# Three fp32 sums over partitions turned into pairs of rounded products, with their splits moved ahead, in an adaLN linear-attention block

## The chip, the cores and the metric

The kernel runs on one NeuronCore of a Trainium2 chip. The metric is the device time of one execution, in microseconds; less is better. Before the change it is 563.58 us, the median of three runs that lie between 562.93 and 564.28.

## What is computed

A block of a transformer with 2048 tokens of width 512: a condition vector `c` gives six modulation vectors; then come a linear attention with 32 heads of width 16 and a bilinear feed-forward of width 1376, each behind a layer norm that is scaled and shifted by its modulation and each added to `x` through a gate (`ga`, `gb`).

```
mod = silu(c) @ w_mod                      # six vectors of 512: sa, ca, ga, sb, cb, gb
h = layernorm(x) * (1 + ca) + sa
q, k, v = h @ wqkv                         # per head
phi(t) = where(t > 0, t + 1, exp(t)) + 1e-6
kv = sum_s phi(k) v ;  z = sum_s phi(k)    # over all tokens
o = (phi(q) kv) / (phi(q) z + 1e-6)
x = x + ga * (o @ wo)
h = layernorm(x) * (1 + cb) + sb
x = x + gb * (((h @ w_gate) * (h @ w_up)) @ w_down)
```

Three of these quantities are sums over the 128 partitions that are wanted as a row, the same on every partition: the gates `ga` (modulation vector 2) and `gb` (vector 5), and `z`.

## The kernel before, in words

Nearly all matrix products run in the type fp32r, which TensorE rounds: each operand is split in a high part (its rounding, made by a copy on ScalarE) and a low part (the difference, made by a subtraction on VectorE), and a product is the sum of three matmuls, high by high, high by low and low by high (`split` L192, `split_raw` L196, `product` L202). A tensor is worked on in tiles of 128 tokens by 512 columns; there are NT = 16 of them in four chunks.

The order of each engine's queue is written out by hand: an instruction stands in its engine's queue where the Python code calls it, and each engine works through its queue in that order. The loop at L612 (`for i in range(4, NT)`) is the key stage. Step i puts in the queues, among other things:

- TensorE: the projection of tile i+2 on the key weights (or, in the last two steps, of tiles 4 and 5 on the query weights), twelve matmuls (`proj` L301, lines 206 to 208); then the twelve matmuls of `t_tile(i)` (L350, lines 355 to 357), which add `x^T phi(k)` of tile i to four banks `tacc` that stay open through the whole loop.
- ScalarE: the high part of the next tile's normalized input (`k_split_x`, L193), the high part of phi(k) of tile i+1 (`k_split`, L346), and two activations on the projection (`phi_a`, L310 and L311).
- VectorE: the two low parts (L194 and L347), the end of phi (`phi_b`, L314), and the running sum of phi(k) over tiles in `zacc` (`z_add`, L338 and L340).
- `extra[i]` (L552 to L562), the work that doesn't belong to the tile: splits of other weights, and the modulation vectors 2 to 5. For one vector, `mod_load` fetches four pieces of `w_mod`, `mod_part` (L547, working in `mod_acc` L166) multiplies each by a column of silu(c) and adds it to an accumulator `accs[v]` on VectorE (L169, L171), and what is left is a sum over the 128 partitions. Vectors 3 and 4 are wanted as columns (`mod_col` L173, eight matmul records with one moving column, then `col_out`). Vectors 2 and 5 are wanted as rows: `mod_row` L184 multiplies a 128x128 matrix of ones by the accumulator in one plain fp32 matmul (L186), which the trace shows as two records, and ScalarE copies the bank (L188).

In the last step, 15, `z` is made in the same way at L654, one fp32 matmul of the ones by `zacc`, and ScalarE adds a constant (L656) to give `zb`. It stands on TensorE between the projection of query tile 5 and `t_tile(15)`; `mod_row(5)` stands behind `t_tile(15)`.

After the loop, VectorE has in its queue: `phi_b` of query tile 5 (L314), two operations on `zb` (L670, L671), two products and sums for the denominators (L676, L682), four operations that finish the four banks `tacc` (L739, from copies by ScalarE at L738), and the four low parts of these (L194). TensorE goes on with the projections of query tiles 6 and 7 and then takes the product of these four tiles with the value weights into `kvps` (L749, lines 206 to 208 with 128 columns).

Buffers come from one pool of 99 tiles that are handed out again when their last reader is done, so that a load or a write can wait for an older tile's reader; loads are all issued in order on the queue of SyncE.

## Time and profile before

| what | value |
|---|---|
| median of three runs | 563.58 us (562.93 to 564.28) |
| the profiled execution, its own time | 561.47 us |
| the profiled execution, span of the instructions | 559.8 us |
| TensorE (PE) busy | 551.9 us, 99% of the span, 2544 instructions |
| VectorE (DVE) busy | 379.8 us, 68% |
| ScalarE (ACT) busy | 294.2 us, 53% |
| GpSimd (POOL) busy | 207.4 us, 37% |
| DMA | 57.24 MB, mean 102 GB/s |

PE and PEld are TensorE's matmuls and weight loads, DVE is VectorE, ACT ScalarE, POOL GpSimd and SP the engine that issues the loads. `L186` is line 186 of the kernel. In a line of the timeline stand the start in us, the duration, the engine, the line and operation, the tile written and the tiles read (without numbers), the shapes, the number of instructions put together, and in brackets how long the engine stood idle before it and what it waited for. Matmuls are pipelined: two of them start 0.23 us apart though each is shown with 0.39 us, so that costs on TensorE are read from starts. The chain of waits goes back from the last instruction, at each step to the one that released it.

### The profile page before, as it was taken

To read this page: it belongs to the slowest core of one execution; us is meant where nothing else is said; L and a number is where in the kernel's file an instruction comes from. 1 tells how busy PE (TensorE), PEld (TensorE's weight loads), DVE (VectorE), ACT (ScalarE), POOL (GpSimd) and SP (SyncE) were. 2 spreads that over 40 slices of the span, in tenths; PEclk is the share of its full clock that TensorE was granted. 3 is DMA by queue.
4 is the path that set the end of the run, shared out by engine and by line. 5 is a ranking of instruction groups with operands and counts; after the bars stand their busy time and mean duration, and the time that the engine had idled before them with its cause. 6 is when DMAs were issued, how large, how long until landed. Compare 5 with 4: busy or idle time off the path is not lost.

```text
span 559.8 us, 7391 instructions
## 1 busy us (share of the span) xinstructions
PE 551.9 (99%) x2544; PEld 453.5 (81%) x2544; DVE 379.8 (68%) x648; ACT 294.2 (53%) x531; POOL 207.4 (37%) x226
## 2 busy tenths in 40 slices
PE   7999999999999999999999999999999999999997
PEld 5888888888888888888888888878888888888775
DVE  5968779869898998865655766862455545444653
ACT  3876858446476877663545355553444334334420
POOL 2000000003327646343556644485424455554200
PEclk9999999999999999999999999999999999999999
DMA  8910224202230020151446136598353211200004
GB/s 254 384 39 1 75 76 150 77 0 71 80 114 2 0 76 0 39 159 68 150 151 195 32 122 221 178 363 286 114 157 87 57 39 48 71 0 1 0 1 150
DMA packets 50133, 57.24 MB, mean 102 GB/s; under 512 B 6384, under 2 KB 28912, under 8 KB 50096
## 3 DMA queue, kind: packets, MB, share of 16 engines
q1 hardware_dynamic: 50096, 56.77, 31.8%
q8 instruction: 20, 0.33, 0.3%
q14 instruction: 17, 0.14, 0.1%
HBM read 43.12 MB, written 13.63 MB: 101 GB/s over the span
## 4 chain that ended last, share of the span: by engine, by line
PE 94%; DVE 3%; DMA 1%; SPq 0%; issue 0%; ACT 0%; POOL 0%
PE bank L970 38%; PE acc L807 8%; PE acc L1048 7%; PE acc L1049 7%; PE acc L1050 7%; PE bank L206 5%; PE bank L207 5%; PE bank L208 5%; PE acc L357 2%; PE acc L355 2%; PE acc L356 2%; PE bank L271 2%; PE acc L439 1%; DMA x<-in_A_x_dram 1%; PE bank L782 1%; PE acc L271 1%
## 5 line engine op out<-in xcount | busy, mean ns | idle before, releaser
L970 PE MATMUL bank<-h,w 128*128 128x512 f32 (+1 forms) x924 | 215.8, 390 | 0.0
L970 PEld LDWEIGHTS bank<-h,w 128*128 128x128 f32 (+1 forms) x924 | 170.8, 185 | 38.6 <-issue 0.4
L976 ACT ACTIVATE bank<-bank 128x512 f32<-128x512 f32 (+1 forms) x44 | 25.6, 581 | 151.2 <-PE bank L970 151.1
L956 POOL TENSOR_TENSOR w<-raw,w 128x256 fp32r<-128x256 f32 (+3 forms) x44 | 46.1, 1048 | 157.2 <-ACT w L949 150.0
L996 DVE TENSOR_TENSOR phi<-bank,g 128x512 f32<-128x512 f32 (+1 forms) x22 | 15.1, 688 | 83.5 <-PE bank L970 79.8
L1048 PE MATMUL acc<-w,kh 128*128 128x512 f32 (+1 forms) x176 | 68.6, 390 | 0.0
L1049 PE MATMUL acc<-w,kh 128*128 128x512 f32 (+1 forms) x176 | 68.6, 390 | 0.0
L1050 PE MATMUL acc<-w,kl 128*128 128x512 f32 (+1 forms) x176 | 68.5, 389 | 0.0
L956 POOL TENSOR_TENSOR w<-t,w 128x512 fp32r<-128x512 f32 (+1 forms) x44 | 57.4, 1305 | 0.0
L1055 DVE TENSOR_TENSOR x<-acc,x 128x512 f32<-128x512 f32 x80 | 50.3, 681 | 8.6 <-PE acc L1050 8.6
L206 PE MATMUL bank<-w,h 128*128 128x512 f32 x112 | 44.8, 400 | 0.0
L208 PE MATMUL bank<-w,h 128*128 128x512 f32 x112 | 43.7, 390 | 0.0
L207 PE MATMUL bank<-w,h 128*128 128x512 f32 x112 | 43.6, 390 | 0.0
L676 POOL TENSOR_TENSOR f<-h,zb 128x512 f32<-128x512 f32 x12 | 17.1, 1439 | 67.8 <-ACT zb L656 49.2
L249 POOL TENSOR_TENSOR rstd<-ve,half 128x4 f32<-128x4 f32 (+3 forms) x12 | 11.2, 930 | 83.0 <-DVE ve L246 71.4
L807 PE MATMUL acc<-w,xh 128*128 128x512 f32 x128 | 40.7, 399 | 0.0
L1048 PEld LDWEIGHTS acc<-w,kh 128*128 128x128 f32 (+1 forms) x176 | 33.0, 188 | 7.1
L1050 PEld LDWEIGHTS acc<-w,kl 128*128 128x128 f32 (+1 forms) x176 | 33.0, 188 | 7.0
L1049 PEld LDWEIGHTS acc<-w,kh 128*128 128x128 f32 (+1 forms) x176 | 33.1, 188 | 6.9
L938 POOL TENSOR_TENSOR t<-raw,t 128x256 f32<-128x256 f32 (+1 forms) x44 | 36.9, 838 | 1.7
L1022 DVE TENSOR_TENSOR g<-bank,u 128x512 f32<-128x512 f32 (+1 forms) x22 | 15.2, 691 | 27.0 <-ACT u L976 27.0
L264 ACT ACTIVATE n<-x,nmr,rstd 128x512 f32<-128x512 f32 x31 | 23.7, 808 | 14.6 <-DVE nmr L254 14.4
(159 smaller groups left out, 1011.3 us busy)
## 6 DMA issues: line engine op xcount, KB each, us to landing
x<-in_A_x_dram SPq DMA_DIRECT2D x24, 256.0 KB, 5.2
raw<-in_w_mod_dram SPq DMA_DIRECT2D x24, 256.0 KB, 3.8
raw<-in_B_w_gate_dram SPq DMA_DIRECT2D x40, 128.0 KB, 3.0
raw<-in_B_w_up_dram SPq DMA_DIRECT2D x40, 128.0 KB, 3.1
raw<-in_B_w_down_dram SPq DMA_DIRECT2D x20, 256.0 KB, 3.1
side_s<-h SPq DMA_DIRECT2D x16, 256.0 KB, 2.5
h<-side_s SPq DMA_DIRECT2D x16, 256.0 KB, 5.5
out_dram<-x SPq DMA_DIRECT2D x16, 256.0 KB, 2.6
```

The costliest lines, as they stand in the source:

```text
L206: nc.tensor.matmul(ps, ah, bh, start=i == 0, stop=False)
L207: nc.tensor.matmul(ps, ah, bl, start=False, stop=False)
L208: nc.tensor.matmul(ps, al, bh, start=False, stop=i == n - 1)
L807: nc.tensor.matmul(yps[i], x, y, start=fresh and k + n == 0, stop=k == KD - 1 and n == 2, skip_group_check=True)
L938: sub = lambda out, x, y: (on or nc.gpsimd).tensor_tensor(out, x, y, op=ALU.subtract)
L956: sub = lambda out, x, y: (on or nc.gpsimd).tensor_tensor(out, x, f32(y), op=ALU.subtract)
L970: mm = lambda x, y, **kw: nc.tensor.matmul(ps, x[:, k], y, skip_group_check=True, **kw)
L976: nc.scalar.activation(out, x, AF.Copy)
L1048: nc.tensor.matmul(dn[j], hh[:n, a:b], dh[:n], start=i == 0, stop=False)
L1049: nc.tensor.matmul(dn[j], hh[:n, a:b], dl[:n], start=False, stop=False)
L1050: nc.tensor.matmul(dn[j], hl[:n, a:b], dh[:n], start=False, stop=i == n_of - 1)
L1055: nc.vector.tensor_tensor(xt, dn[j], xt, op=ALU.add)
```

## The change

It replaces the three fp32 matmuls by pairs of fp32r ones. A 128x128 matrix of ones in fp32r, `ones_r`, is made once near the start, by a VectorE copy from a column of ones (`ones` shrinks to that column). Each of the three accumulators is split in high and low like any other operand, and `over_rows` adds ones times high and ones times low in one bank. The split of vector 2 stands in step 10 (its matmuls stay in step 11), that of `zacc` in step 14, behind the last `z_add`, and that of vector 5 in step 13 (its matmuls stay in step 15); the pieces of vector 5 are worked off one earlier each (piece 0 in step 12, pieces 1 to 3 in step 13), and the first of the four `wo` tiles is split in step 13 and not in step 14. The column sums are the same instructions as before.

```diff
-    ones = consts.tile([P, P], F32, name="ones")
+    ones = consts.tile([P, 1], F32, name="ones")
     nc.gpsimd.memset(ones, 1.0)
+    ones_r = consts.tile([P, P], F32R, name="ones_r")
...
-            nc.tensor.matmul(ps[:, b:b + 1], acc[:, b * P:(b + 1) * P], ones[:, 0:1], start=True, stop=True)
+            nc.tensor.matmul(ps[:, b:b + 1], acc[:, b * P:(b + 1) * P], ones, start=True, stop=True)
...
-    def mod_row(v, acc):
+    def over_rows(ps, pair):
+        for m, x in enumerate(pair):
+            nc.tensor.matmul(ps, ones_r, x, start=m == 0, stop=m == 1)
+
+    def mod_row(v, pair):
         ps = bank()
-        nc.tensor.matmul(ps, ones, acc, start=True, stop=True)
+        over_rows(ps, pair)
...
     n0.stats(0)
+    nc.vector.tensor_copy(ones_r, ones.to_broadcast([P, P]))
     silu()
...
-             10: lambda: (mod_part(3, 0, 1, 2), mod_load(5)),
+             10: lambda: (accs.update({2: split_raw(accs[2])}), mod_part(3, 0, 1, 2), mod_load(5)),
              11: lambda: (mod_part(3, 3), mod_part(4, 0, 1), rows.update({2: mod_row(2, accs[2])})),
-             12: lambda: (raw_o.extend(load(wo_v[k], "raw") for k in range(KD)), mod_part(4, 2, 3), cols.update({3: col_out(3, mod_col(accs[3], bank()), 0.0)})),
-             13: lambda: (mod_part(5, 0, 1, 2), cols.update({4: col_out(4, mod_col(accs[4], bank()), 1.0)})),
-             14: lambda: (mod_part(5, 3), wo_s.extend(split_raw(x) for x in raw_o)), 15: lambda: rows.update({5: mod_row(5, accs[5])})}
+             12: lambda: (raw_o.extend(load(wo_v[k], "raw") for k in range(KD)), mod_part(4, 2, 3), mod_part(5, 0), cols.update({3: col_out(3, mod_col(accs[3], bank()), 0.0)})),
+             13: lambda: (mod_part(5, 1, 2, 3), wo_s.extend(split_raw(x) for x in raw_o[:1]), accs.update({5: split_raw(accs[5])}), cols.update({4: col_out(4, mod_col(accs[4], bank()), 1.0)})),
+             14: lambda: (wo_s.extend(split_raw(x) for x in raw_o[1:]),), 15: lambda: rows.update({5: mod_row(5, accs[5])})}
...
         if i + 1 < NT:
             z_add(i + 1)
+        if i + 1 == NT - 1:
+            zpair = split_raw(zacc)
...
             zps = bank()
-            nc.tensor.matmul(zps, ones, zacc, start=True, stop=True)
+            over_rows(zps, zpair)
```

More of the change, by code (lines that the diff above doesn't have):

```diff
@@ L398, in block_one @@
         at = at_of(v, b)
-        nc.tensor.matmul(sums_in(b)[:, at:at + 1], sums[v, b // 2][:, b % 2 * P:(b % 2 + 1) * P], ones[:, 0:1],
+        nc.tensor.matmul(sums_in(b)[:, at:at + 1], sums[v, b // 2][:, b % 2 * P:(b % 2 + 1) * P], ones,
                          start=True, stop=True)
```

## The prediction

> **What bounds the kernel now.** I read the page first (the span and the shares of the chain of waits), then the chain in order of time around the three sums, then the timeline there, engine by engine.

> ```profile
> span 559.8 us, 7391 instructions
> PE 94%; DVE 3%; DMA 1%; SPq 0%; issue 0%; ACT 0%; POOL 0%
> ```

> By the page TensorE sets the end nearly everywhere, so that TensorE time saved is time saved. But 3% of the chain is VectorE's, about 17 us, and the question of this change is whether its three sums lie inside or outside of that. The chain in order of time answers it (start, duration, what):

> ```profile
> 125.61 0.24 PE bank L208
> 125.85 0.02 issue
> 125.87 0.61 ACT h L310
> 126.50 0.64 ACT h L311
> 127.16 0.69 DVE h L314
> ...
> 132.13 2.65 DVE n L739 x4
> 134.78 2.42 DVE w L194 x4
> 137.20 0.04 issue
> 137.25 0.33 PE bank L207
> ```

> From 125.85 to 137.25 us the chain leaves TensorE: the projection of query tile 5 ends, ScalarE and then VectorE finish it (L310, L311, L314), VectorE does the operations on `zb` and on the four banks without a pause, and TensorE's product into `kvps` (137.25) takes up the last low part. What TensorE does in these 11.4 us is beside the chain. Two of the three sums are there, as the timeline shows:

> ```profile
> 103.59 0.39 PE L357 MATMUL acc<-kl,xh 128*128 128x512 f32 x1
> 103.82 1.02 PE L186 MATMUL bank<-f,ones 128*128 128x512 f32 x2
> ...
> 107.44 0.39 PE L355 MATMUL acc<-kh,xh 128*128 128x512 f32 x1
> ...
> 122.72 0.39 PE L357 MATMUL acc<-kl,xh 128*128 128x512 f32 x1
> ...
> 125.67 1.02 PE L654 MATMUL bank<-z,ones 128*128 128x512 f32 x2
> ...
> 129.30 1.02 PE L186 MATMUL bank<-f,ones 128*128 128x512 f32 x2
> ```

> The row for vector 2 (103.82) is before 125.85, on the chain; the one for z (125.67, behind the last L208 of that projection) and the one for vector 5 (129.30) are behind it. In the waits of the weight loads stands how close TensorE is to VectorE there:

> ```profile
> PEld bank L207 <- DVE w L194: 0.4, 2, 0.2
> ```

> TensorE arrives at `kvps` only some 0.4 us too early. Whatever it gains between 125.85 and 137 beyond what VectorE gains turns into more of this wait.

> **The price of one sum.** From the last matmul of `t_tile` to the first one behind the next projection: with the fp32 sum between, 103.59 to 107.44, 3.85 us; without one, 122.72 to 125.67, 2.95 us, which is 13 starts of 0.227. So an fp32 sum takes 0.90 us of TensorE (the slightly longer starts behind it included). Its replacement has the shape of every other matmul here, 128x128 by 128x512 in fp32r: two starts, 0.45 us. No row shows such a matmul with `ones_r`. Its bounds are 0.45 (two ordinary ones) and 0.90 (no faster than now); I take 0.45, since all the fp32r matmuls in the 2.95 us above start 0.227 apart. **Saved: 0.45 us per sum, 1.35 us in all on TensorE, of which 0.45 is on the chain.**

> **What VectorE and ScalarE must do for it.** Each split adds a ScalarE copy and a VectorE subtraction:

> ```profile
> L193 ACT ACTIVATE w<-raw 128x512 fp32r<-128x512 f32 x32 | 19.5, 625 | 4.9 <-DVE raw L1065 4.8
> L194 DVE TENSOR_TENSOR w<-raw,w 128x512 fp32r<-128x512 f32 x32 | 21.5, 684 | 5.7 <-ACT w L193 4.2 <-issue 1.5
> 104.00:125.67 21.67, 21.67 (x102) 17.75 (x102) 15.72 (x28) 9.99 (x17) 0.00 (x0) 1.00 0.00 0
> ```

> That is 3 x 0.63 = 1.9 us of ScalarE and 3 x 0.68 = 2.1 us of VectorE. The last line is the stretch from the first sum to the second: in 21.67 us VectorE is busy 15.72, ScalarE 9.99, POOL 0.00 and the DMA share is 0.00. There is room on average; what counts is the order in the queues, with these idle times in brackets:

> ```profile
> 99.38 0.73 ACT L346 ACTIVATE kh<-phi,eps_phi 128x512 fp32r<-128x512 f32 x1 [1.46 <-DVE phi L314]
> 108.94 0.69 DVE L314 SCALAR_TENSOR_TENSOR phi<-bank,phi 128x512 f32<-128x512 f32 x1 [1.56 <-ACT phi L311]
> 115.33 0.69 DVE L314 SCALAR_TENSOR_TENSOR phi<-bank,phi 128x512 f32<-128x512 f32 x1 [2.38 <-ACT phi L311]
> 117.05 1.54 DVE L171 SCALAR_TENSOR_TENSOR f<-raw,sc,f 128x512 f32<-128x512 f32 x2
> 120.43 0.60 ACT L310 ACTIVATE h<-bank 128x512 f32<-128x512 f32 x1 [3.65 <-PE bank L208]
> 121.72 0.69 DVE L314 SCALAR_TENSOR_TENSOR h<-bank,h 128x512 f32<-128x512 f32 x1 [1.86 <-ACT h L311]
> 123.59 2.49 DVE L194 TENSOR_TENSOR w<-raw,w 128x512 fp32r<-128x512 f32 x4
> 125.87 0.60 ACT L310 ACTIVATE h<-bank 128x512 f32<-128x512 f32 x1 [2.10 <-PE bank L208]
> 127.16 0.69 DVE L314 SCALAR_TENSOR_TENSOR h<-bank,h 128x512 f32<-128x512 f32 x1 [1.08 <-ACT h L311]
> ```

> *Split of vector 2 (step 10).* Its high part goes into ScalarE's idle 1.46 us ahead of 99.38. Its low part pushes VectorE's queue by 0.60 until the idle 1.56 us at 108.94 swallows it. Its matmuls come at 103.8, three microseconds later. Cost nothing; without those idle times 0.6.

> *Split of vector 5 (step 13).* This is the tightest place. ScalarE's copy stands ahead of the next tile's high parts and of L310 and waits for three multiply-adds of VectorE. With everything 0.45 earlier than before, L314 starts at 114.88 (not 115.33), `z_add` at 115.5, and the three L171 (0.74 each) end at 118.3. Until then ScalarE stands still where it now has 3.65 us idle. Then it does the high part and the two for tile 15 (0.63, 0.62, 0.72, with overlaps) until 120.1, and L310 of query tile 4, which TensorE allows at 120.43 - 0.45 = 119.98, is 0.1 late. The low parts of tile 15 come at 121.0 and are used at 125.7.

> *Split of z (step 14).* VectorE's L314 follows at 121.4, the last `z_add` ends at 122.7, ScalarE's high part at 123.35, VectorE's low part at 124.05; then the three `wo` splits that are left (0.60 apart as at 123.59, one of the four having gone to step 13) keep ScalarE until 124.95 and VectorE until 125.85. The pair for z is due at 125.67 - 0.45 = 125.22: 1.2 us spare. L310 of query tile 5 is due at 125.42 and L314 at 126.71: spare are 0.47 us on ScalarE and 0.86 on VectorE. So the start of VectorE's 10 us is set by TensorE, as now, and moves by 0.45 alone. Cost nothing; were the 0.47 used up, each further microsecond on ScalarE would be one at the end.

> *From there on.* `zb` is made by ScalarE's next instruction behind L311 (126.50), and stays there: its bank is filled well before. VectorE's stretch keeps its length, and ends 0.45 earlier. TensorE reaches `kvps` 1.35 earlier and waits 0.4 + 0.9 = 1.3 us.

> *The start.*

> ```profile
> 1.50 0.44 DVE L148 CAST w<-f 128x512 fp32r<-128x512 f32 x1
> 4.63 0.18 DVE L238 BATCH_NORM_AGGREGATE mv<-st 128x2 f32<-128x6 f32 x1
> 6.08 0.69 DVE L237 BATCH_NORM_STATS2 st<-x 128x6 f32<-128x512 f32 x1 [0.81 <-DMA x<-in_A_x_dram]
> ```

> The copy that makes `ones_r` stands behind 4.63. No row has its shape; between nothing and the 0.44 of a cast four times as wide, I take 0.15 to 0.2. VectorE waits 0.81 us for data at 6.08, so it is hidden at either end; without that wait it would cost its own length.

> *Loads and buffers.* No load is added and SyncE's order is the same. Six more tiles from the pool change whose reader the last loads of `w_mod` and the four of `wo` wait for (now, for two of them, the low part of vector 2 and the multiply behind it, by my count of VectorE's queue near 101 us); their first use is in step 12, behind the L314 at 108.94.

> ```profile
> 98.57 1.78 SPq L110 DMA_DIRECT2D raw<-in_A_wo_dram  x4
> ```

> They are issued from 98.57 to 100.35 and the last would be some 1 us later; the first `wo` split comes behind the L314 of 115.33, the others at 123. Nothing.

> **Sum.** -0.45 us: the span 559.8 becomes 559.35, the profiled execution's own time (1.67 more, 561.47) 561.02. That execution was 2.1 us under the median of the runs, so the difference is put on the median: 563.58 - 0.45 = **563.1 us**. It is 0.08%, and about 0.2% (1.13 us) is what a measurement of this kernel can tell from no change.

> **Rivals.**

> *All three count.* If VectorE's stretch shortened with TensorE's, the gain would be 1.35: 562.2 us. For it speak the chain's 94% and a 0.4 us wait so small that it may be an artefact; against it that VectorE has no gap in its stretch and starts it from L311.

> *The pair is no cheaper than fp32.* Then nothing is gained, 563.6 us. For it: no row shows it; against it, every fp32r matmul here.

> *ScalarE's queue becomes the bound (slower).* The mechanism is the wait in step 13: ScalarE stands before the high part of vector 5, and behind it stand tile 15's high parts and the two projections' L310. It decides from 0.47 us of delay on. If the two later splits ran one after the other with nothing beside them, 2 x (0.63 + 0.68) = 2.6 us would be added; less 0.47 and less the 0.45 gained, that is +1.7: 565.3 us. For it: ScalarE is blocked for 3.5 us in this step. Against: VectorE and ScalarE have their idle times in these very places, and POOL and DMA are silent there.

> *The clock closes.* The first matmuls of the execution are slower than the later ones:

> ```profile
> L153 PE MATMUL acc<-w x20: 388/582/793, 2.0 to 9.9; 128*128 128x512 f32 x20
> 2.00 6.55 PE L153 MATMUL acc<-w 128*128 128x512 f32 x18 [2.00 <-DVE w L148]
> ```

> 18 of them take 6.55 us where 18 x 0.227 = 4.1 would do: 2.5 us. If the longer wait at `kvps` brought that state back, 563.1 + 2.5 = 565.6 us. Against it: a wait of 0.4 didn't, and the 1.3 us comes in several pieces. [...]

> **How the numbers follow.** Forecast 0.63 (563.1); all three 0.14 (562.2); pair no cheaper 0.08 (563.6); ScalarE's queue 0.12 (565.3); clock 0.03 (565.6). Faster by over 0.2% means under 562.45: the second case and a little of the first by the spread of medians, 0.19. Slower means over 564.71: the last two, 0.14. Between: 0.67. The range takes the first three cases with the spread of the runs, +-0.7 us, about the likeliest, and 0.1 below the full gain: 562.1 to 564.2; the slow cases, 0.15, are left out.

> **What would show it.** Each sum as two matmuls with 0.23 between starts; L310 of query tile 5 at 125.4; VectorE without a gap from 126.7 to 136.75; `kvps` waiting for L194 for about 1.3 us, not 0.4; the same order of events 0.45 earlier from then on. I am wrong if L310 of tile 5 waits for ScalarE and not for the projection, if VectorE's stretch is shorter than 10 us, or if the pair takes other than 0.45.

## The result, and the profile after

| | before | after |
|---|---|---|
| median of 22 runs each, us | 562.91 (560.85 to 564.65) | 567.81 (560.53 to 570.24) |
| ratio of the runs after to those before | | 1.0058, 95% interval 1.0037 to 1.0078 |
| profiled execution: own time, span, us | 561.47, 559.8 | 567.49, 565.8 |
| mean granted clock of it | 1.000 | 0.988 |

The change makes the kernel slower, by 4.9 us of the medians. The ratio is smaller than the medians say, because executions more than 1.5% above the fastest, four of the 22 (569 us and more) and one each of `d_some` and `a_shift5` below, are left out of it as if they were disturbed, though they show the same fall of the clock as the others. The 22 executions fall into two groups: 17 with a mean clock of 0.990 or less (median 568.5), and five with more (median 562.1, 0.8 under before).

The page of the kernel after, its span, the granted clock in 40 slices, and the shares of the chain:

```profile
span 565.8 us, 7393 instructions
PEclk9899999999799999999999999999999999999999
PE 92%; DMA 4%; DVE 2%; SPq 0%; issue 0%; ACT 0%; POOL 0%
```

The third row is as dull as before. The second has a 7 in its eleventh slice, 141 to 156 us (40 slices of 14.1 us). What stands there in the timeline is the product into `kvps`. First what went as forecast, in the timeline from 126 us (start, duration, engine, line; in brackets the idle time before it and what ended it):

```profile
126.28 0.62 PE L187 MATMUL bank<-w,ones_r 128*128 128x512 f32 x2
126.47 0.60 ACT L315 ACTIVATE h<-bank 128x512 f32<-128x512 f32 x1 [0.52 <-PE bank L213]
126.73 0.39 PE L360 MATMUL acc<-kh,xh 128*128 128x512 f32 x1
127.77 0.69 DVE L319 SCALAR_TENSOR_TENSOR h<-bank,h 128x512 f32<-128x512 f32 x1 [0.84 <-ACT h L316]
129.45 0.62 PE L187 MATMUL bank<-w,ones_r 128*128 128x512 f32 x2
129.90 0.39 PE L211 MATMUL bank<-w,h 128*128 128x512 f32 x1
130.10 0.60 ACT L193 ACTIVATE row<-bank 128x512 f32<-128x512 f32 x1 [1.78 <-PE bank L187]
135.32 2.49 DVE L199 TENSOR_TENSOR w<-n,w 128x512 fp32r<-128x512 f32 x4
```

Each pair takes 0.45 us of TensorE (126.28 to 126.73, 129.45 to 129.90). ScalarE still waits for the projection of query tile 5 (0.52 us to spare), VectorE for ScalarE (0.84). Then the waits of the weight loads (us in total, how often, the longest):

```profile
PEld bank L212 <- DVE w L199: 1.3, 4, 0.8
PEld bank L978 <- DMA h<-side_s: 0.9, 2, 0.6
```

The first is the wait at `kvps`, 0.4 us before. Now the same two microseconds by two in both kernels (the stretch, TensorE's busy time and matmuls, the granted clock, DMA). Before:

```profile
134.00:136.00 2.00, 2.00 (x12) 1.00 0.14 33
136.00:138.00 2.00, 1.90 (x15) 1.00 0.90 224
138.00:140.00 2.00, 2.00 (x21) 1.00 0.94 238
```

After:

```profile
134.00:136.00 2.00, 1.56 (x8) 1.00 0.30 77
136.00:138.00 2.00, 1.79 (x10) 1.00 0.89 231
138.00:140.00 2.00, 2.00 (x14) 0.67 0.79 215
140.00:142.00 2.00, 2.00 (x11) 0.50 0.01 2
142.00:144.00 2.00, 2.00 (x11) 0.50 0.00 0
144.00:146.00 2.00, 2.00 (x10) 0.50 0.00 0
146.00:148.00 2.00, 2.00 (x7) 0.50 0.54 163
148.00:150.00 2.00, 2.00 (x8) 0.77 0.58 210
```

A busy share of 100% hides it: the clock is halved from 138.7 to 148.9 us (two parts of 1.3 and 0.9 us, and 8 us between, 10.2 in all), and matmuls that only take longer count as busy. The count in brackets gives it away: 21 matmuls in two microseconds before, 11 after. One sees it on single instructions too, in the product's 128-column matmuls:

```profile
135.34 0.22 PE L211 MATMUL bank<-w,w 128*128 128x128 f32 x1
136.06 0.33 PE L212 MATMUL bank<-w,w 128*128 128x128 f32 x1 [0.50 <-DVE w L199]
...
138.25 0.27 PE L212 MATMUL bank<-w,w 128*128 128x128 f32 x1
138.37 0.27 PE L213 MATMUL bank<-w,w 128*128 128x128 f32 x1
...
140.20 0.41 PE L211 MATMUL bank<-w,w 128*128 128x128 f32 x1
140.41 0.42 PE L212 MATMUL bank<-w,w 128*128 128x128 f32 x1
```

They start 0.11 apart at 138.3 and 0.21 apart at 140.3. What it costs is read from one instruction in both traces, behind the product: ScalarE's copy for query tile 8. Before, with vector 5's copy of 130.10 above beside it:

```profile
130.35 0.60 ACT L188 ACTIVATE row<-bank 128x512 f32<-128x512 f32 x1 [2.65 <-PE bank L186]
144.53 0.60 ACT L310 ACTIVATE h<-bank 128x512 f32<-128x512 f32 x1 [1.43 <-PE bank L208]
```

After:

```profile
150.00 0.60 ACT L315 ACTIVATE h<-bank 128x512 f32<-128x512 f32 x1 [3.09 <-PE bank L213]
```

From 0.25 us early (130.10 against 130.35) to 5.47 us late (150.00 against 144.53): 5.7 us are lost in these twenty microseconds. 0.9 is the longer wait, as forecast; the rest, **4.8 us, is the clock**. Another 0.5 us comes at 387 us, the wait for `side_s` above; it is in some kernels' profiles and not in others' (below, at the end of the account).

Both kernels also lose some clock in the first 25 us, in some executions and not in others. So offsets between the two traces hold one random term: ScalarE's first copy behind the warm-up stands at 20.35 us before and at 21.40 after, 1.05 later, since this execution of the kernel after had the half clock there for 3.4 us (15.79 to 19.20) and that of the kernel before had the full one:

```profile
20.35 0.78 ACT L410 ACTIVATE h<-bank,both 128x512 fp32r<-128x512 f32 x1 [1.71 <-DVE both L403]
```

```profile
21.40 0.78 ACT L415 ACTIVATE h<-bank,both 128x512 fp32r<-128x512 f32 x1 [2.91 <-DVE both L408]
```

### The profile page after: what moved, and what is told of

Same layout as the page of the kernel before. It is cut to its first block, busy times and chain, and to the rows that moved or that the text cites. A ratio compares the mean times of both kernels' runs of the same rounds, so it can differ in the third digit from the quotient of the medians.

```text
span 565.8 us, 7393 instructions
## 1 busy us (share of the span) xinstructions
PE 556.9 (98%) x2544; PEld 458.6 (81%) x2544; DVE 381.1 (67%) x652; ACT 296.2 (52%) x534; POOL 206.9 (37%) x226
## 4 chain that ended last, share of the span: by engine, by line
PE 92%; DMA 4%; DVE 2%; SPq 0%; issue 0%; ACT 0%; POOL 0%
PE bank L978 35%; PE acc L815 8%; PE acc L1056 7%; PE acc L1057 7%; PE acc L1058 7%; PE bank L211 5%; PE bank L212 5%; PE bank L213 5%; PE acc L362 2%; PE acc L360 2%; PE acc L361 2%; DMA h<-side_s 2%; PE acc L444 2%; PE bank L276 2%; DMA x<-in_A_x_dram 1%; PE bank L790 1%
## 5 line engine op out<-in xcount | busy, mean ns | idle before, releaser
L684 POOL TENSOR_TENSOR f<-h,zb 128x512 f32<-128x512 f32 x12 | 17.1, 1438 | 72.7 <-ACT zb L664 48.7
L269 ACT ACTIVATE n<-x,nmr,rstd 128x512 f32<-128x512 f32 x31 | 23.7, 808 | 14.3 <-DVE nmr L259 14.1
```

## The experiments

Two numbers are given for each kernel beside its time. The clock is said to close where the granted clock falls to half. The idle time is what TensorE stands still from 130 to 152 us, the stretch less its busy time in the sum row of the windows view (132 to 156 us for the four kernels that are shifted). The number of closings is how many executions had a mean clock of 0.990 or less: 10.2 us at half of 566 takes 0.009 off the mean. None of 127 executions of the kernel before, run beside them, came to that (lowest 0.991, once).

| kernel | median, us | ratio, 95% | idle at `kvps`, us | closings |
|---|---|---|---|---|
| after | 567.81 | 1.0058, 1.0037 to 1.0078 | 0.65 | 17 of 22 |
| b_again | 562.34 | 0.9997, 0.998 to 1.0013 | 0.11 | 0 of 12 |
| a_fill6 | 563.17 | 1.0004, 0.9987 to 1.0021 | 0.00 | 0 of 12 |
| z_row5 | 568.34 | 1.0086, 1.0059 to 1.0113 | 0.67 | 7 of 8 |
| row2 | 561.80 | 0.9984, 0.9967 to 1.0000 | 0.10 | 0 of 12 |
| stall1 | 564.61 | 1.0032, 1.0008 to 1.0055 | 0.59 | 3 of 12 |
| stall2 | 564.61 | 1.0024, 1.0005 to 1.0043 | 0.58 | 1 of 12 |
| a_half | 562.12 | 0.9979, 0.9959 to 1.0000 | 0.00 | 1 of 12 |
| b_half | 561.55 | 0.9972, 0.9950 to 0.9995 | 0.00 | 0 of 12 |
| d_late | 561.17 | 0.9969, 0.9944 to 0.9994 | 0.10 | 0 of 10 |
| b_late | 562.39 | 0.9977, 0.9951 to 1.0003 | 0.00 | 0 of 10 |
| row2_late | 562.00 | 0.9969, 0.9945 to 0.9994 | 0.00 | 0 of 10 |
| stall4 | 570.28 | 1.0128, 1.0078 to 1.0179 | 1.75 | 4 of 4 |
| stall25 | 565.43 | 1.0037, 1.0018 to 1.0055 | 0.79 | 3 of 10 |
| d_some | 567.17 | 1.0056, 1.0018 to 1.0094 | 0.57 | 7 of 10 |
| a_shift5 | 564.58 | 1.0033, 1.0005 to 1.0061 | 0.65 | 4 of 12 |
| a_shift10 | 568.31 | 1.0104, 1.0070 to 1.0139 | 0.67 | 3 of 6 |
| a_shift15 | 569.54 | 1.0112, 1.0061 to 1.0163 | 1.35 | 3 of 6 |
| stall25_shift | 570.93 | 1.0125, 1.0082 to 1.0169 | 0.79 | 5 of 6 |

The kernel before, run beside them, had medians of 562.66 (b_again to row2), 562.98 (stall1 to b_half), 563.39 (d_late to stall4), 562.61 (stall25, d_some) and 562.74 (the last four).

A mean clock of 0.989 or 0.990 doesn't say where the clock was halved. Every closing at `kvps` that a profile shows lasted 10.2 us or more, and executions with one take some 6 us more than the same kernel's at 0.996 and above (`after`, `d_some`; half clock at the start is part of it). The executions at 0.989 and 0.990 of `stall1`, `stall2`, `a_half` and `stall25` take only 2 to 4 us more, so that their closings may have been others. With a limit of 0.988 these four kernels have none, and the other counts stay, but for one execution less of `after` and of `stall4`.

### Which sum does it, and is it the wait?

My theory on seeing the result was that the wait of 1.3 us at `kvps` closes the clock. The rivals: one of the pairs, or the splits and loads that were moved. `b_again` is the kernel before, unchanged:

> The kernel before once more, for the granted clock of each of its executions. Clock theory (the longer wait at kvps makes the granted clock fall to half there): the mean clock of the executions is 1.000 or 0.997 (at most one window of 3.4 us at half clock, at the start), never 0.99 or less, and the time is 561 to 564 us. Rival (the clock falls at random places in either kernel, and the change merely met it): some executions of this kernel have 0.99 or less too.

`a_fill6` is the kernel after with six dense matmuls put in front of the product, into its own bank; the product overwrites what they leave.

```
     kvps = bank()
+    for _ in range(6):
+        nc.tensor.matmul(kvps, wo_s[0][0][:, :P], wo_s[0][0], start=True, stop=True)
```

> The changed kernel with six needless matmuls (128x128 by 128x512, fp32r) into the bank of kvps ahead of the product, 6 x 0.227 = 1.36 us of TensorE, which is what the change freed before that place. They change no result. Clock theory: TensorE no longer waits longer than before the change, the clock stays at full there, and the time is 561 to 563 us, about 0.998 of before. Rival (the new splits in the queues of ScalarE and VectorE hold things up): the six matmuls help nothing, 567 to 568 us. If the matmuls were on the path: 1.4 us more than the changed kernel.

`row2` is the kernel before with vector 2 alone as a pair; `z_row5` the kernel after with vector 2 as an fp32 sum again, so that z and vector 5 alone are pairs:

```
 def over_rows(ps, pair):
+    if not isinstance(pair, tuple):
+        nc.tensor.matmul(ps, f32(ones_r), pair, start=True, stop=True)
+        return
...
-             10: lambda: (accs.update({2: split_raw(accs[2])}), mod_part(3, 0, 1, 2), mod_load(5)),
+             10: lambda: (mod_part(3, 0, 1, 2), mod_load(5)),
```

> The other part alone: vector 2 as a pair with its split in step 10, z and vector 5 in fp32 and step 12 to 14 as before. Clock theory: the wait at kvps is as before (0.4 us), the clock stays, and the time is 0.45 us under before: 562.5 us, 0.999 of before. Rival (any fp32 sum less makes the clock fall): 567.

> The changed kernel with vector 2 summed in one fp32 matmul again and its split left out; z and vector 5 stay pairs. Clock theory: TensorE is still 0.9 us earlier at kvps and waits 1.3 us, the clock falls, 567 to 568.5 us. Rival that it is the whole time freed ahead of kvps wherever it lies: about as much, but by the sum of my prediction 0.45 more than the changed kernel.

`b_again` had no closing in 12 (mean clocks of 0.994 to 0.998, where 0.997 at the least had been expected), so that a fall in the middle isn't something that the kernel before has at random. The loss goes with z and vector 5 (568.34, clock closed in 7 of 8); vector 2's pair alone brings no loss and perhaps a small gain (561.8 against 562.66, an interval that ends at 1.0000). In the waits of `z_row5`, and of `row2`, in this order:

```profile
PEld bank L215 <- DVE w L202: 1.3, 4, 0.8
```

```profile
PEld bank L215 <- DVE w L202: 0.4, 2, 0.2
```

With the six matmuls in the gap TensorE does 1.36 us more and the kernel is 4.6 us faster than after (563.17, a little over the 561 to 563 expected): no closing in 12. Those 1.36 us mostly take the place of the wait. That speaks for the wait, but the six matmuls also bring other work.

### The wait made longer in the kernel before, and the gap filled with real work

`stall1` and `stall2` are the kernel before, fp32 sums and all, with one sum of VectorE done twice and three times, which lengthens its stretch ahead of `kvps`:

```
-        nc.vector.reduce_sum(den0, zb.rearrange("p (h i) -> p h i", i=DH), axis=AX.X)
+        for _ in range(2):    # 3 in stall2
+            nc.vector.reduce_sum(den0, zb.rearrange("p (h i) -> p h i", i=DH), axis=AX.X)
```

> The kernel before, untouched but for one more sum over zb on VectorE (the same sum into den0 twice) ahead of the four operations on tacc: 0.60 us more on VectorE's stretch, so that TensorE waits 1.0 us at kvps and not 0.4; its sums stay in fp32. Clock theory: the granted clock falls at 138 to 140 us in part or most of the executions, and the median rises by more than the 0.6 us: 564 to 568. Rival (only fewer fp32 sums or the new splits bring the loss): 0.6 us more than before, 563.3.

> The same with two more sums: 1.2 us more on VectorE, TensorE waits 1.6 us, more than in the changed kernel (1.3). Clock theory: the clock falls in nearly all executions, 1.2 + 5 us: 568 to 570, mean clock 0.985 to 0.99. Rival: 1.2 us more, 563.9, with the clocks of before.

`a_half` and `b_half` are the kernels after and before with the first six matmuls of query tile 8's projection put ahead of the product instead of behind it:

```
+    ps8 = bank()
+    part8(0, 1)
     kvps = bank()
...
-    ps = proj(8, wq)
+    part8(2, 3)
+    ps = ps8
```

> The changed kernel with useful work in the wait: the first six of the twelve matmuls of query tile 8's projection stand ahead of the product into kvps, the other six where they were. Clock theory: TensorE waits no longer than before the change, the clock stays; VectorE's stretch ends 0.45 earlier and 1.36 us of TensorE's work behind it is gone: 0.5 to 1.8 us under before, 561 to 562 us. Rival (splits): 567.

> The same reordering in the kernel before. TensorE then comes to kvps 1 us after VectorE and doesn't wait; what is gained is at most the 0.4 us that it waited: 562.3 to 562.7, 0.999 to 1.0 of before. If it gained as much as in the changed kernel, the gain there would be the reordering's and not that of the pairs.

Filling the gap with work that has to be done anyway helps both kernels, and takes the changed one from 1.0058 to 0.9979. The kernel before gained as much (0.9972, where 0.999 at best had been expected), so that what `a_half` is under before can be the reordering's alone. But the stalls disappoint. They wait as long as the kernel after, 1.3 us in four pieces, the longest 0.7 us; and `stall2` waits no longer than `stall1`, since behind its third sum the scaling of den0 took 0.43 us, where it had taken 1.16 in `stall1`. Yet at most 4 of 24 executions closed. Either 0.59 us of idle time lies just under a step and 0.65 just above it, or the wait isn't all.

### The wait taken away, and made much longer

`d_late`, `b_late` and `row2_late` are the kernels after, before and `row2` with the two operations of `den_z` moved from ahead of the states' splits to behind query tile 8's sums:

```
-    den_z()
     den_p(1, 0, 1)
...
     den_a(0, 2, on=nc.vector)
+    den_z()
     ps = proj(8, wq)
```

`stall4` is `stall1` with the sum done five times.

> The changed kernel with the sum of z over heads and its scaling (den0: 0.68 and 0.65 us on VectorE at 128.38 and 129.09) moved from ahead of the four states' splits to behind query tile 8's sums, where nothing waits for them. Nothing else differs, and no matmul is added or moved. Theory (the wait of 1.3 us at the kv product closes the clock): the splits end some 1.2 us earlier, the waits of the weight loads for the split at the kv product fall from 1.3 us to 0.2 or less, the clock doesn't fall there in any execution (no mean clock of 0.990 or less in more than 1 of 12), and the median is 561.5 to 562.7, a ratio to the kernel before of 0.996 to 0.9995. Rival (the pairs or the other moved splits close the clock, whatever the wait): the clock falls in most executions still, 567 us.

> The kernel before with the same move of den0, its fp32 sums kept. Theory: its wait at the kv product of 0.4 us goes to about nothing, and the clock had been full there, so 0.2 to 0.4 us are saved: 562.2 to 562.6, a ratio of 0.998 to 1.000; the difference to the changed kernel with this move is the three sums' own saving, up to 0.45 us on the path. Rival: no change at all, since those 0.4 us come back at the next wait.

> Vector 2's sum alone as a pair, and den0 moved. Theory: 0.45 us from the pair and 0.2 to 0.4 from the wait add up: 561.4 to 562.3, a ratio of 0.997 to 0.999, no closing at the kv product. Rival: the two overlap and it is the same as either.

> The kernel before with den0's sum over heads done five times on VectorE ahead of the states' splits: four more of 0.68 us (0.6 apart), some 2.4 us, of which up to 0.4 is taken back where VectorE no longer shares its time with GpSimd. The fp32 sums stay as before. Theory (length of the wait decides): the wait at the kv product is 2.5 us or more, in place of the 1.3 us with which the clock closed in a minority of executions, and the clock is halved there in most executions: mean clock 0.991 or less in 9 or more of 12, median 568 to 571. Rival (the wait isn't enough by itself; the pair sums or the changed order are needed): mean clock 0.991 or less in at most 4 of 12, and the median is 2 us above the kernel before, 565.

With the pairs kept and 1.2 us of VectorE taken out of the way, the wait in `d_late` is that of the kernel before (not under 0.2 us, as I had expected), and the clock stays full:

```profile
PEld bank L212 <- DVE w L199: 0.4, 2, 0.2
```

It has the lowest median of the study, 0.9969 of the kernel before, as has `row2_late`; `b_late` without the pairs has 0.9977, so that the three sums' own 0.4 us is not shown by these intervals. With the fp32 sums kept and a wait of 2.3 us (2.5 or more had been expected), `stall4` closed in all of its four executions:

```profile
PEld bank L207 <- DVE w L194: 2.3, 4, 1.7
```

```profile
138.00:140.00 2.00, 1.72 (x10) 1.30 (x10) 2.00 (x5) 1.94 (x5) 0.00 (x0) 1.00 0.91 218
140.00:142.00 2.00, 2.00 (x12) 2.00 (x13) 2.00 (x3) 0.43 (x1) 1.44 (x2) 0.61 0.58 167
142.00:144.00 2.00, 2.00 (x11) 2.00 (x11) 1.07 (x2) 0.00 (x0) 2.00 (x2) 0.50 0.00 0
```

(The second stretch has the clock at 0.61: TensorE, weight loads, VectorE, ScalarE and GpSimd stand between the length and it.) So a wait there is enough without any pair, and without the wait the pairs do no harm. What wasn't explained was the middle.

### Idle time alone does not decide

`stall25` has three sums and one over half the width, the fp32 sums kept; `d_some` is `d_late` with one and a half useless sums put back in the old place, the pairs kept.

```
+    nc.vector.reduce_sum(den0[:, :NH // 2], zb[:, :D // 2].rearrange("p (h i) -> p h i", i=DH), axis=AX.X)
+    nc.vector.reduce_sum(den0, zb.rearrange("p (h i) -> p h i", i=DH), axis=AX.X)    # three times in stall25
```

> The kernel before, its fp32 sums kept, with den0's sum over heads done three times and once more over half its width, ahead of the states' splits. From 130 to 152 us TensorE stood still 0.10 us in the kernel before, 0.59 and 0.58 with the sum done two and three times, 0.65 in the changed kernel, 1.75 with the sum done five times. Expected here 0.8 to 1.0 us, by half a sum (0.3 us) more than three. Theory (TensorE's idle time at the kv product alone decides, and the step lies near 0.6): mean clock 0.990 or less in 8 or more of 12, median 567 to 569. Rival (with the fp32 sums kept, 0.9 us is still too little; the changed kernel closes at 0.65 because of its pair sums): at most 4 of 12, as with two and three sums, median 565.

> The changed kernel, its pairs kept, with den0's sum and scaling moved behind query tile 8 as in the kernel that moved them (idle 0.10 us), and one and a half such sums, 0.9 us, put in the old place with no use. So TensorE's idle time at the kv product is between: 0.3 to 0.4 us, under the 0.59 with which a minority of executions closed. Theory (idle time alone decides): mean clock 0.990 or less in at most 2 of 12, median 561.5 to 563. Rival (with the pair sums the clock closes at less idle time than with the fp32 ones): 4 or more of 12, median 563.5 to 567.

The theory that idle time alone decides fell. The sum rows of the windows from 130 to 152 us, of `stall25` and of `d_some`:

```profile
sum 22.00, PE 21.21; mean PE 1.93
```

```profile
sum 22.00, PE 21.43; mean PE 1.95
```

0.79 us of idle time closed the clock in at most 3 of 10, and 0.57 in 7 of 10. (`d_some` got more idle time than the 0.3 to 0.4 us meant for it, so that it isn't the small dose it was to be; against `stall25` it decides all the same.)

### Where the wait falls on the clock's grid

| kernel | idle, us | first matmul of `kvps`, us | behind the edge, us | fewest columns in a window | clock closed |
|---|---|---|---|---|---|
| after | 0.65 | 135.34 | 0.09 | 2176 | at 138.67 |
| d_some | 0.57 | 135.18 | 0.20 | 2176 | at 138.39 |
| z_row5 | 0.67 | 136.86 | 0.54 | 2688 | at 139.74 |
| a_shift15 | 1.35 | 138.17 | 0.98 | 2944 | at 140.61 |
| stall1 | 0.59 | 138.00 | 1.07 | 3328 | no |
| stall25 | 0.79 | 138.89 | 1.70 | 3328 | no |
| stall2 | 0.58 | 136.47 | 1.89 | 3328 | no |
| a_shift10 | 0.67 | 137.78 | 1.96 | 3328 | no |
| a_shift5 | 0.65 | 135.61 | 1.99 | 3328 | no |
| stall4 | 1.75 | 136.28 | 2.66 | 1792 | at 140.45 |
| stall25_shift | 0.79 | 139.48 | 2.92 | 2560 | at 143.39 |

In these profiles the clock falls at the end of the window that holds the wait, or most of it, when less than 1 us of the dense projection before it is in the same window. In the five with 1.1 to 2.0 us of the projection in the window first, it stays full, though most of the idle time lies in one window there too. Three windows of the profile after, and two of `stall25`, show it (the stretch, TensorE's busy time and matmuls, the granted clock, DMA):

```profile
131.84:135.26 3.42, 3.42 (x17) 1.00 0.01 1
135.26:138.67 3.41, 2.76 (x19) 1.00 0.85 221
138.67:142.08 3.41, 3.41 (x18) 0.50 0.31 86
```

```profile
137.18:140.59 3.41, 2.72 (x15) 1.00 0.64 161
140.59:144.01 3.42, 3.32 (x28) 1.00 0.54 147
```

TensorE is busy for 2.76 us in the window behind which the clock falls and for 2.72 in that of `stall25` behind which it doesn't, so that busy time doesn't set the two apart. The columns do: 17 matmuls of 128 start in the first, 2176 columns, and 7 of 512 and 6 of 128 in the second, 4352 (the counts in brackets take in two more that started before). In the table the clock fell behind windows of 1792 to 2944 columns and behind none of 3328. From 20 to 550 us of the profile before, the window with the fewest has 3328 (136.44 to 139.85, at `kvps`) and the clock stays full; in that after, the window of 2176 is the only one at full clock with fewer than 5632. In the first 20 us the count doesn't tell: the clock stayed full behind a window with 1416 columns (10.15 to 13.56, before) and behind one with 2568 (8.96 to 12.38, after), and fell behind one with 2444 (12.38 to 15.79, after). The count was found in these profiles, no run was made to test it by itself, and the first 20 us show that it is no rule for other places. In the profile of the kernel before, any stretch of 3.41 us at `kvps`, wherever the grid lay, would have 3072 columns or more; in those of `stall1`, `stall25`, `a_shift5` and `a_shift10` half of the places of the grid, or a little more, would give a window of 2944 or fewer (0.50, 0.48, 0.54 and 0.56).

The last four runs were made to test that the place counts. Three are the kernel after with 5, 10 and 15 more matmuls (1.14, 2.27 and 3.41 us, a third, two thirds and the whole of a window) in vector 2's bank near 105 us; its pair overwrites them. TensorE sets the end there, so that everything behind was to come later and nothing else to change. The fourth is `stall25` with vector 2's fp32 sum done three times, 1.8 us.

```
+        for _ in range(5 if v == 2 else 0):    # 10, 15
+            nc.tensor.matmul(ps, ones_r, pair[0], start=True, stop=True)
         over_rows(ps, pair)
```

> The changed kernel with five more matmuls in vector 2's bank at about 105 us, ahead of its pair, which overwrites them; TensorE sets the end there, so that everything behind it comes 5 x 0.227 = 1.14 us later, the wait at the kv product is the same, and the idle time stays 0.65 us. What it changes is where the wait falls on the grid of 3.41 us on which the clock's changes lie in every profile (in the changed kernel the half clock begins at 138.67, which is 36 times 3.413 us behind its first fall at 15.79). Theory (the clock falls when one such window holds the whole wait and what follows of the 128-column matmuls, so that the place of the wait on the grid counts, and the start of the execution, which depends on the same grid, makes that place anything but random): the share of executions with a mean clock of 0.990 or less falls from 17 of 22 to 40% or less, and the median is 563 to 566, below the 567.8 of the changed kernel although TensorE does 1.14 us more. Rival (pair sums lower the threshold, and the place doesn't count): 70% or more still, median 568 to 569.

> The same with ten more matmuls, 2.27 us. Theory: the place of the wait has moved by two thirds of a window; the share with 0.990 or less is again clearly under the changed kernel's, 20 to 60%. Rival: 70% or more, median 569 to 570.

> The same with fifteen more matmuls, 3.41 us, one whole window. Theory: the wait falls on the same place of the grid as in the changed kernel, so that the share with 0.990 or less is as there, 65% or more, and the median 570 to 572: 3.4 us and the full price of the clock. Rival (any later place is harmless): a share of 40% or less, median under 567.

> The kernel before with two and a half more sums of den0 ahead of the splits (3 of 10 executions with 0.990 or less, idle time 0.80 us), and vector 2's fp32 sum done three times, which puts everything behind it 2 x 0.90 = 1.8 us later. In the profiles its wait lay some 1.1 us behind an edge of the grid, that of the kernels that closed 0 to 0.7 us. Theory: the wait comes to where the changed kernel's is; the share with 0.990 or less rises from 3 of 10 to 60% or more, and the median is 568 to 571. Rival (with the fp32 sums this wait closes the clock only now and then, wherever it lies): 40% or less, 566.5 to 568.

`a_shift5` has 1.14 us more of TensorE's work and is 3.2 us faster than the kernel after: 4 closings of 12, where it had 17 of 22, with the same wait:

```profile
PEld bank L214 <- DVE w L201: 1.3, 4, 0.8
```

And the fp32 kernel's wait, moved by 1.8 us, closed the clock in 5 of 6 instead of at most 3 of 10:

```profile
PEld bank L208 <- DVE w L195: 1.5, 4, 0.9
```

Both speak for the place and against the pairs. `a_shift10` is where the theory put it (3 of 6). `a_shift15` should have been back at two thirds or more, and had 3 of 6, which is neither: of six executions no more can be read, in either, and the wait of `a_shift15` isn't the same. In its profile a multiplication of VectorE took 1.86 us (L686 at 132.49), where the same took 0.68 in the profile after (L684 at 129.65), and the idle time is 1.35 us and not 0.65.

## Why the prediction was wrong

- **The price of the sums: right.** 0.45 us for a pair, at all three places; the five executions in which the clock didn't close have a median of 562.1, 0.8 under the kernel before, where 0.45 less was forecast (five executions between 560.5 and 564.0 can't tell the two apart).
- **The splits on ScalarE and VectorE: right, nearly to the digit.** L310 of query tile 5 (now L315) at 126.47, which is 125.42 without the 1.05 us of the start, forecast 125.4; spare 0.52 and 0.84 us, forecast 0.47 and 0.86. VectorE's stretch goes without a gap from 127.77 to 137.8, 10 us as before. ScalarE's queue did not become the bound.
- **What becomes of the 0.9 us that z and vector 5 gain: right.** They turn into wait; 1.3 us at `kvps`, forecast 1.3.
- **The step that failed** is that this wait costs nothing more than itself: "Against it: a wait of 0.4 didn't, and the 1.3 us comes in several pieces." Exactly that rival came, and it had been given 0.03. The runs showed that the pieces add up: the clock closed in 17 of 22 executions, with 0.65 us of idle time in the profiled one, in four pieces with 128-column matmuls half as dense between them (0.11 us apart, where those of 512 are 0.23 apart). That several pieces, and a wait of 0.4 us that had cost nothing, spoke against it was an estimate of mine, and no run bears it out. In the window from 135.26 to 138.67, which holds them, TensorE was busy for 81% by the profile's modelled ends; it took up 2176 columns, 28% of the 7680 of the window before it.
- **Its price was mis-sized as well**: 2.5 us, from 18 warm-up matmuls, against 4.8 us measured. The starts agree: matmuls of 512 columns are 0.43 us apart in the warm-up (2.59 to 6.43, profile before, whose clock records begin behind that, at 6.73) and 0.43 at half clock behind the product (145.85 to 148.84, after). The length doesn't: at `kvps` the half clock outlasted the wait. In the profile after its three windows have 2048, 2432 and 4096 columns, and the clock is full again behind the third; the product's 128-column matmuls, themselves slowed to 0.21 us apart, last until 145.1, so that they fill the first two.
- **"The same order of events 0.45 earlier from then on" was wrong** from 138.67 us on: 5.47 later at query tile 8.
- The forecast treated TensorE's surplus as harmless; `d_late` shows what had to go with it, 1.2 us less of VectorE's work ahead of the states' splits.

What stays open: each kernel has one profile, so that the place on the grid was seen for one execution each, and the shares of closings were only moved by it, not computed from it: they differ from the half of the places that the columns give, and what sets the place in one execution isn't known: that the start of an execution goes with the grid, as I had it ahead of `a_shift5`, no run shows. What happens between 2944 and 3328 columns, and between 0.1 and 0.57 us of idle time, wasn't tried. The wait of 0.3 to 1.1 us for `side_s` near 380 us is in twelve of the twenty profiles (`b_half`, without any pair, among them) and not in those of the kernel before, `b_again`, `b_late`, `d_late`, `a_shift5` and the stalls but `stall4` and `stall25_shift`; its cause isn't known.

## What to carry to other kernels

When a faster engine runs into a wait, price not only the wait but what it may do to the clock (here 0.9 us and 4.8 us): look whether the wait lies beside narrow matmuls, count the columns that TensorE takes up in each few microseconds there, and fill the wait, with work that has to be done anyway (`a_half`, `b_half`) or by taking work out of the other engine's way (`d_late`). When a profile has TensorE busy all the time and is still slower, read the granted clock and the number of matmuls in each stretch; a single profile, or a median that hides two groups of executions, can tell the wrong story.

## What the runs showed of the hardware

- In four profiles (`after`, `d_some`, `z_row5`, `stall25_shift`) idle times of TensorE of 0.57 to 0.79 us in all, no piece over 0.64 us, were followed by a clock halved for 10.2 us; in five others (`stall1`, `stall2`, `stall25`, `a_shift5`, `a_shift10`) 0.58 to 0.79 us were not. They lay on different places of the grid of 3.41 us. The price was 4.8 us in the profile after.
- At `kvps` the clock fell behind each of the six windows of that grid in which the matmuls took up 1792 to 2944 columns, and stayed full where the fewest were 3328 (the five others, and the kernel before); a window of the projections has 7680.
- The place counted beside the length: 1.14 us of useless matmuls 30 us earlier took the closings from 17 of 22 to 4 of 12 and the median from 567.8 to 564.6.
- By their clock records, which begin at 6.73 us in the profile before and at 5.55 in that after, sixteen of the twenty profiles have 3.4 or 6.8 us at half clock in the first 25 us, four none, and the kernel before has one of each kind (`b_again`, 3.4 us); the times go with the mean clock: in one set of 35 executions 560.6 to 561.6 us at 1.000, 562.0 to 563.7 at 0.997, 563.9 to 565.5 at 0.994, all of the kernel before.
- A sum of VectorE done once more cost 0.6 us, or next to nothing: the same scaling of 128x32 elements behind it took 0.18 to 1.16 us, by where it fell.
